# Layer 2 in token blocks of 1024 instead of 768

## The chip, the cores and the metric

One core of a Trainium2 chip. TensorE (PE) multiplies matrices and adds into the eight banks of PSUM, each 512 fp32 wide per partition; VectorE (DVE) and ScalarE (ACT) read PSUM and SBUF; GpSimd (POOL) works in SBUF; SyncE (SP) issues the DMAs. The metric is the device time of the whole program in microseconds, as the median of several runs.

## What is computed

A filter in the frequency domain, then two dense layers on the 6016 filtered tokens of 256 features. The change is in the second layer:

```python
y   = irfft(rfft(x, axis=1) * (filt_r + 1j * filt_i))     # (2, 3008, 256) -> 6016 tokens
h   = y @ w_in;   x2 = (h * sigmoid(h)) @ w_out           # layer 1: 256 -> 2048 -> 256
g   = x2 @ w_gate; v = x2 @ w_val                         # layer 2: 256 -> 1536, twice
out = (g * sigmoid(g) * v) @ w_out2                       # 1536 -> 256
```

Every fp32 operand is cut into a high and a low part (type fp32r), and a product is three matmuls: high·high, high·low, low·high.

## The kernel before

The program is written out instruction by instruction in Python; the engines keep that order, and semaphores and buffers follow from it. Layer 1 ends at about 640 us; the rest is layer 2.

Layer 2 walks over blocks of `STEP2` = 768 tokens (seven of them and one of 640), and in a block over six **units** (`Pair`, line 666), each with 256 hidden features of gate and value. In a unit, gate (`Gate` g) and value (v) are each computed by seven products instead of eight, on halves of the tokens and quarters of the weights: `p15` (products 1 and 5, into banks `a` and `b`), `p6` (into bank `y`), product 2 (onto `a`), `p3` (onto `b`), `p7` and `p4` (onto `y`). So a unit is 14 products, 42 matmuls (line 616) whose moving operand is half a block wide: 384 columns, or 320 in the last block. The order of a unit on PE is g1, g5, the p4 of the unit before's v, g6, g2, g3, g7, v1, v5, g4, v6, v2, v3, v7. Between them ACT copies `a` and `b` aside (lines 639, 641), takes Silu (690, 694, 699) and makes the high part of the hidden values `h` (711, 738); DVE adds and multiplies (647, 651, 656, 664, 686, 707, 709) and makes the low part of one half of them (714); POOL adds (660) and makes the low part of the other (739).

The hidden values go through `w_out2` in the **out products** (`m2_out`, line 744): one for each 128 tokens and part, 256 columns wide (line 756), added over the whole block in banks `acc`, two token tiles to a bank, so three banks for 768 tokens. They stand in a queue (`queue`), first in first out, and are dealt out evenly behind the matmuls of the products: `owed[1]` is the queue's length at the start of a unit over 42. The last unit of the program is dealt out at double rate in its second part, and `finish` (line 718) ends it in two halves.

All banks come from one pool of eight. With three for `acc`, five are left for `a`, `b` and `y` of the gates.

The operands of the products: `load_x2` reads a block, `prep_x2` makes four sums of its quarters on POOL (line 593), and `split_x2` makes high and low parts of seven operands on ACT and DVE (lines 606, 607), into ten buffers of the pool `late2`; the next block's are made while the last units of a block run. The general pool `mid` has 35 buffers of 4 KB per partition: weights, `h`, `s`, and so on.

```python
for k, (wpart, xpart) in enumerate(PARTS):
    nc.tensor.matmul(o, w_op(u, key, n, wpart), x[:, xpart, :size2(t) // 2], ...)
    owed[0] += owed[1]
    while owed[0] >= 1 and queue:
        owed[0] -= 1
        drain(len(queue) - 1)
```

Of the kernel before, what the change touches and what calls it, by code (L numbers as in the profile page):

```python
# [11 lines left out]
F32R = mybir.dt.float32r  # L12
# [16 lines left out]
P = 128  # L29
# [1 line left out]
NTOK = B * N  # L31
NBLK = -(-NTOK // 512)

STEP2 = 768
NBLK2 = -(-NTOK // STEP2)
CHUNK = 4 * N2

# [57 lines left out]
def fft_filter_mlp_kernel(  # L95
# [56 lines left out]
    def mid(shape, name, dtype=F32):  # L152
        return mp.tile(shape, dtype, tag="mid", name=name)
# [415 lines left out]
    xop, late2, x2_of = {}, {}, {}  # L569

    def size2(t):
        return min(STEP2, NTOK - STEP2 * t)

    def load_x2(t):

        r0, m = STEP2 * t, size2(t)
        xs = [mid([P, STEP2], "x2") for _ in range(2)]
        a = r0
# [10 lines left out]
    def prep_x2(t, part):  # L589

        x, n = x2_of[t], size2(t) // 2
        r = mid([P, 2, STEP2 // 2], "xr")
        sub = lambda o, a, b: nc.gpsimd.tensor_tensor(o, a, b, op=ALU.subtract)
# [8 lines left out]

    def split_x2(t, k):
        v, n = x2_of[t][k], size2(t) // 2
        x = late2["p"].tile([P, 2, STEP2 // 2], F32R, tag="x", name="xo", bufs=10)
        nc.scalar.copy(x[:, 0, :n], v)
        nc.vector.tensor_tensor(x[:, 1, :n], v, x[:, 0, :n], op=ALU.subtract)
        xop[t, k] = x
# [236 lines left out]
    for n, k in enumerate((1, 5, 6, 2, 3, 7, 4)):  # L845
        at(END1 - 8 + n, split_x2, 0, k)
# [11 lines left out]
    for t in range(1, NBLK2):  # L858
        u = 6 * t - 6
        later(u + 2, 0, load_x2, t)  # L860
        later(u + 3, 1, prep_x2, t, 0)
        later(u + 3, 3, prep_x2, t, 1)
        for k, n in ((0, 1), (1, 5), (3, 6)):
            later(u + 4, k, split_x2, t, n)

        for k, n in ((3, 2), (3, 3), (4, 7)):
            later(u + 5, k, split_x2, t, n)
        later(u + 6, 0, split_x2, t, 4)
# [241 lines left out]
```

## Time and profile before

| | us |
|---|---|
| median of 3 runs (1189.18 to 1190.61) | 1189.54 |
| span of the profiled execution | 1187.3 |
| PE busy in it | 1176.4 |
| DVE / ACT / POOL busy | 724.4 / 667.3 / 432.6 |

The profile page gives busy time by engine, the chain of work that ended last, and the costliest groups of instructions. The trace behind it is asked for stretches of time, for one engine's instructions in order, and for who waited for whom. PE's rows show a start that was measured and an end that is modelled, so that rows of matmuls overlap; from one start to the next is what a matmul costs.

### The profile page before, as it was taken

What the parts mean: (1) busy time and instruction counts of PE and PEld (TensorE: products, weight loads), DVE (VectorE), ACT (ScalarE), POOL (GpSimd) and SP (SyncE); (2) the same over time, 40 slices, a digit from 0 to 9 for tenths busy, and PEclk for the clock granted to TensorE, in tenths of its full rate; (3) what the DMA queues carried; (4) which work ended last, traced back from release to release, by engine and by line L of the source; (5) the groups of instructions that cost most, each with busy time, mean ns of one, the idle gap of its engine ahead of it and who ended that gap; (6) DMA issues with size and microseconds to landing.
All of it is one profiled execution on the core that took longest, in us unless ns stands there. A gap on an engine that the chain in (4) does not pass through costs nothing.

```text
span 1187.3 us, 17740 instructions
## 1 busy us (share of the span) xinstructions
PE 1176.4 (99%) x6646; PEld 1059.2 (89%) x6646; DVE 724.4 (61%) x1078; ACT 667.3 (56%) x1208; POOL 432.6 (36%) x341
## 2 busy tenths in 40 slices
PE   9999999999999999999999999999999999999998
PEld 7578788888888888888899999999999999999998
DVE  4778866763433433443345676767777676767766
ACT  3778766655565565656554554555545455454553
POOL 2556632420144134134211424334343343434332
PEclk9999999999999999999999999999999999999999
DMA  9883523313034232312563514242341434223230
GB/s 221 249 250 80 143 87 92 106 63 98 1 107 134 88 119 97 114 57 95 190 245 134 190 63 166 93 142 92 106 135 60 160 107 143 89 90 138 72 134 23
DMA packets 67574, 141.57 MB, mean 119 GB/s; under 512 B 5568, under 2 KB 32704, under 8 KB 67488
## 3 DMA queue, kind: packets, MB, share of 16 engines
q1 hardware_dynamic: 67488, 140.44, 36.8%
q8 instruction: 52, 0.85, 0.3%
q14 instruction: 34, 0.28, 0.1%
HBM read 104.50 MB, written 35.91 MB: 118 GB/s over the span
## 4 chain that ended last, share of the span: by engine, by line
PE 92%; DVE 2%; POOL 2%; ACT 2%; DMA 2%; issue 1%; SPq 0%; POOLq 0%; DVEq 0%; ACTq 0%
PE h L509 20%; PE acc L553 20%; PE acc L756 16%; PE y L616 13%; PE xa L616 8%; PE xb L616 8%; PE s L342 2%; PE s L175 2%; PE s L178 2%; DMA fr<-in_fr_dram 1%; DVE h L517 1%; DMA raw<-in_w_out_dram 1%; POOL fl L200 1%; POOL m L413 1%; PE s L229 1%
## 5 line engine op out<-in xcount | busy, mean ns | idle before, releaser
L756 PE MATMUL acc<-w,h 128*128 128x256 f32 x1692 | 465.5, 280 | 0.5 <-POOL h L714 0.2
L756 PEld LDWEIGHTS acc<-w,h 128*128 128x128 f32 x1692 | 316.0, 188 | 1.1 <-POOL h L714 0.4
L517 DVE TENSOR_TENSOR h<-u,h 128x512 fp32r<-128x512 f32 (+1 forms) x192 | 167.5, 876 | 244.7 <-ACT h L516 244.3
L553 PE MATMUL acc<-h,w 128*128 128x512 f32 (+1 forms) x1152 | 293.0, 387 | 1.8 <-ACT h L516 1.6
L509 PE MATMUL h<-xh,w 128*128 128x512 f32 (+1 forms) x768 | 269.5, 392 | 0.7 <-DVE xl L356 0.7
L553 PEld LDWEIGHTS acc<-h,w 128*128 128x128 f32 x1152 | 215.6, 188 | 45.9 <-ACT h L516 2.0
L536 ACT ACTIVATE u<-h 128x512 f32<-128x512 f32 (+1 forms) x192 | 112.8, 588 | 132.9 <-PE h L509 132.4
L616 PE MATMUL y<-xo,wst 128*128 128x384 f32 (+1 forms) x576 | 174.6, 336 | 0.0
L616 PE MATMUL xb<-xo,wst 128*128 128x384 f32 (+1 forms) x576 | 173.8, 335 | 0.0
L509 PEld LDWEIGHTS h<-xh,w 128*128 128x128 f32 x768 | 144.1, 188 | 30.5 <-DVE xl L356 1.2
L616 PE MATMUL xa<-xo,w 128*128 128x384 f32 (+1 forms) x576 | 164.1, 335 | 0.0
L660 POOL TENSOR_TENSOR c<-u,s 128x384 f32<-128x384 f32 (+1 forms) x95 | 97.5, 1026 | 173.5 <-DVE u L656 135.0
L739 POOL TENSOR_TENSOR h<-c,h 128x768 fp32r<-128x768 f32 (+1 forms) x47 | 85.8, 1826 | 176.2 <-ACT h L738 173.1
L509 PE MATMUL h<-xl,w 128*128 128x512 f32 (+1 forms) x384 | 149.2, 389 | 0.0
L516 ACT CAST h<-u 128x512 fp32r<-128x512 f32 (+1 forms) x192 | 117.5, 612 | 6.2
L616 PEld LDWEIGHTS y<-xo,wst 128*128 128x128 f32 x576 | 107.3, 188 | 0.8 <-DVE u L647 0.2
L616 PEld LDWEIGHTS xb<-xo,wst 128*128 128x128 f32 x576 | 107.4, 188 | 0.0
L616 PEld LDWEIGHTS xa<-xo,w 128*128 128x128 f32 x576 | 101.6, 188 | 0.0
L711 ACT CAST h<-ga 128x768 fp32r<-128x768 f32 (+1 forms) x48 | 39.5, 823 | 100.4 <-DVE ga L709 100.4
L664 DVE TENSOR_TENSOR c<-y,s 128x384 f32<-128x384 f32 (+1 forms) x96 | 52.1, 543 | 71.2 <-PE y L616 71.2
L509 PEld LDWEIGHTS h<-xl,w 128*128 128x128 f32 x384 | 72.1, 188 | 14.8
L714 DVE TENSOR_TENSOR h<-ga,h 128x768 fp32r<-128x768 f32 (+1 forms) x47 | 70.3, 1496 | 21.4 <-ACT h L711 21.4
(105 smaller groups left out, 1490.9 us busy)
## 6 DMA issues: line engine op xcount, KB each, us to landing
wst<-ds_g SPq DMA_DIRECT2D x48, 512.0 KB, 3.5
wst<-ds_v SPq DMA_DIRECT2D x48, 512.0 KB, 3.4
raw<-in_w_out_dram SPq DMA_DIRECT2D x14, 512.0 KB, 6.9
zt<-d SPq DMA_DIRECT2D x16, 384.0 KB, 5.2
x<-in_xp_dram SPq DMA_DIRECT2D x15, 384.0 KB, 8.8
d<-z SPq DMA_DIRECT2D x11, 512.0 KB, 3.9
d<-x SPq DMA_DIRECT2D x22, 256.0 KB, 2.2
out_dram<-ob SPq DMA_DIRECT2D x21, 256.0 KB, 2.2
```

The costliest lines, as they stand in the source:

```text
L509: nc.tensor.matmul(ps[:, :n], wt[key, f // 4, g][:, wpart, o:o + P], x[xpart][:, g, :n], start=(g == 0 and k == 0), stop=(g == 1 and k == 2),)
L516: nc.scalar.copy(h[:, 0, :n], u[:, :n])
L517: nc.vector.tensor_tensor(h[:, 1, :n], u[:, :n], h[:, 0, :n], op=ALU.subtract)
L536: nc.scalar.activation(u[:, :n], ps[:, :n], AF.Silu)
L553: nc.tensor.matmul(a[:, :n], w[:, wpart, o:o + 128], h[:, xpart, :n], start=(f == 0 and k == 0), stop=(f == 15 and k == 2),)
L616: nc.tensor.matmul(o, w_op(u, key, n, wpart), x[:, xpart, :size2(t) // 2], start=(first and k == 0), stop=(last and k == 2), skip_group_ch ...
L660: eng.tensor_tensor(self.c[:, self.n:], u3, self.s[:, 1], op=ALU.add)
L664: nc.vector.tensor_tensor(self.c[:, :self.n], self.y, self.s[:, 0], op=ALU.add)
L711: nc.scalar.copy(h[0], a[:, :m])
L714: eng.tensor_tensor(h[1], a[:, :m], h[0], op=ALU.subtract)
L739: nc.gpsimd.tensor_tensor(h[1], c, h[0], op=ALU.subtract)
L756: nc.tensor.matmul(a[:, D * (i % 2):D * (i % 2) + D], h[hpart][:, P * i:P * i + P], w[:, wpart, f % 2], start=(at_ == 0 and k == 0 and i % ...
```

## The change

`STEP2` becomes 1024, so layer 2 has five blocks of 1024 tokens and one of 896: 36 units instead of 48. Products become 512 columns wide (448 in the last block), and a block has four `acc` banks, so four banks are left for the gates. A buffer of `xo` grows from 3 KB to 4 KB; two of the seven operands (1 and 5) move to the pool `mid`, and `late2` keeps eight buffers. No other line changes; line numbers behind line 605 grow by three.

```diff
-STEP2 = 768
+STEP2 = 1024
...
     def split_x2(t, k):
         v, n = x2_of[t][k], size2(t) // 2
-        x = late2["p"].tile([P, 2, STEP2 // 2], F32R, tag="x", name="xo", bufs=10)
+        if k in (1, 5):
+            x = mid([P, 2, STEP2 // 2], "xo", F32R)
+        else:
+            x = late2["p"].tile([P, 2, STEP2 // 2], F32R, tag="x", name="xo", bufs=8)
```

**The first out products.** PE's order in the second unit of layer 2, before: `xa`, `xb` and `y` are the banks of the gates, `acc<-h` at line 553 is the end of layer 1, `acc<-w_5103,h` at line 756 the first out products, the second of which reads the low part of the first unit's `h`.

```order
L616 MATMUL xb<-xo,wst 128x384 x3
L616 MATMUL y<-xo,w_5080 128x384 x3
L553 MATMUL acc<-h,w 128x384
L616 MATMUL y<-xo,wst 128x384 x2
L553 MATMUL acc<-h,w 128x384
L616 MATMUL y<-xo,wst 128x384
L616 MATMUL xa<-xo,w_5039 128x384
L756 MATMUL acc_5569<-w_5103,h 128x256
L616 MATMUL xa<-xo,w_5039 128x384 x2
L756 MATMUL acc_5569<-w_5103,h 128x256
```

The same place now:

```order
L619 MATMUL xb<-xo,wst 128x512 x3
L619 MATMUL y<-xo,w_5080 128x512
L553 MATMUL acc<-h,w 128x384
L619 MATMUL y<-xo,w_5080 128x512 x2
L553 MATMUL acc<-h,w 128x384
L619 MATMUL y<-xo,wst 128x512
L759 MATMUL acc_5561<-w_5103,h 128x256
L619 MATMUL y<-xo,wst 128x512 x2
L759 MATMUL acc_5561<-w_5103,h 128x256
```

The second out product stands three products' matmuls earlier, behind 15 instead of 18 since the first unit's v3.

**The out products between the products.** PE in the middle of layer 2, before: one out product at most follows a product's matmul.

```order
L616 MATMUL xa<-xo,w_5686 128x384 x2
L756 MATMUL acc_7196<-w_5566,h 128x256
L616 MATMUL xa<-xo,w_5686 128x384
L756 MATMUL acc_7196<-w_5566,h 128x256
L616 MATMUL xb<-xo,wst 128x384
```

And now:

```order
L619 MATMUL y<-xo,w_5497 128x512
L759 MATMUL acc_7348<-w_5123,h 128x256 x2
L619 MATMUL y<-xo,w_5497 128x512
L759 MATMUL acc_7348<-w_5123,h 128x256
L619 MATMUL y<-xo,w_5497 128x512
```

A unit has 48 out products to 42 matmuls, where it had 36; six times a unit two out products follow each other.

**The end.** PE's last rows, before: `h` through `w_5762` is the last unit's first half, through `w_5827` from the fourth row on what `finish` makes.

```order
L756 MATMUL acc_11174<-w_5762,h 128x256 x6
L756 MATMUL acc_11175<-w_5762,h 128x256 x6
L756 MATMUL acc_11176<-w_5762,h 128x256 x3
L756 MATMUL acc_11175<-w_5827,h 128x256 x3
L756 MATMUL acc_11176<-w_5827,h 128x256 x3
L756 MATMUL acc_11174<-w_5827,h 128x256 x6
L756 MATMUL acc_11175<-w_5827,h 128x256 x3
```

And now, with seven token tiles instead of five:

```order
L759 MATMUL acc_9962<-w_5779,h 128x256 x6
L759 MATMUL acc_9963<-w_5779,h 128x256 x6
L759 MATMUL acc_9964<-w_5779,h 128x256 x6
L759 MATMUL acc_9965<-w_5779,h 128x256 x3
L759 MATMUL acc_9964<-w_5849,h 128x256 x6
L759 MATMUL acc_9965<-w_5849,h 128x256 x3
L759 MATMUL acc_9962<-w_5849,h 128x256 x6
L759 MATMUL acc_9963<-w_5849,h 128x256 x6
```

The last half of `h` is first read 30 out products behind the start of these rows, where it was 21.

## Rows read from the trace of the kernel before

**Rows 1.** Page: PE's busy time, and the chain that ended last, by engine.

```profile
PE 1176.4 (99%) x6646; PEld 1059.2 (89%) x6646; DVE 724.4 (61%) x1078; ACT 667.3 (56%) x1208; POOL 432.6 (36%) x341
...
PE 92%; DVE 2%; POOL 2%; ACT 2%; DMA 2%; issue 1%; SPq 0%; POOLq 0%; DVEq 0%; ACTq 0%
```

**Rows 2.** Waits of PE from 640 us: us in total, times, longest.

```profile
PE acc L756 <- POOL h L714: 0.2, 1, 0.2
```

**Rows 3.** Stretches of layer 1 and 2: length, busy (x instructions), granted clock, DMA.

```profile
300.00:590.00 290.00, 290.00 (x1333) 239.68 (x1332) 114.31 (x177) 175.07 (x312) 97.84 (x84) 1.00 0.30 98
...
700.00:1100.00 400.00, 400.00 (x2679) 398.69 (x2678) 286.80 (x451) 202.53 (x366) 157.38 (x128) 1.00 0.34 114
```

**Rows 4.** PE groups by shape, of 300 to 590 and 700 to 1100 us: busy, mean ns.

```profile
L342 PE MATMUL s<-cst,zt 96*128 96x94 f32 x136 | 17.5, 271 | 0.0
...
L756 PE MATMUL acc<-w,h 128*128 128x256 f32 x1236 | 345.3, 279 | 0.0
```

**Rows 5.** PE in order of time, layer 2: start us, modelled us.

```profile
799.88 0.28 PE L756 MATMUL acc<-w,h 128*128 128x256 f32 x1
800.00 0.34 PE L616 MATMUL y<-xo,wst 128*128 128x384 f32 x1
...
801.93 0.34 PE L616 MATMUL xb<-xo,wst 128*128 128x384 f32 x1
```

**Rows 6.** PE in order of time, layer 1: small matmuls, and 512 columns.

```profile
396.05 1.03 PE L342 MATMUL s<-cst,zt 96*128 96x94 f32 x8
396.87 0.48 PE L509 MATMUL h<-xh,w 128*128 128x512 f32 x1
...
500.08 0.40 PE L509 MATMUL h<-xh,w 128*128 128x512 f32 x1
500.31 1.53 PE L553 MATMUL acc<-h,w 128*128 128x512 f32 x6
```

**Rows 7.** PE in order of time, last block of layer 2, 320 columns.

```profile
1139.72 0.31 PE L616 MATMUL xb<-xo,wst 128*128 128x320 f32 x1
...
1141.20 0.31 PE L616 MATMUL xa<-xo,w 128*128 128x320 f32 x1
```

**Rows 8.** All engines in order of time, from unit 0's v3 to the second out product.

```profile
638.04 0.33 PE L616 MATMUL xb<-xo,wst 128*128 128x384 f32 x1
...
639.60 0.84 ACT L711 CAST h<-ga 128x768 fp32r<-128x768 f32 x1 [2.29 <-DVE ga L709]
...
640.47 1.54 DVE L714 TENSOR_TENSOR h<-ga,h 128x768 fp32r<-128x768 f32 x1 [0.44 <-ACT h L711]
...
642.25 0.28 PE L756 MATMUL acc<-w,h 128*128 128x256 f32 x1
```

**Rows 9.** Groups by shape from 860 us: busy us, mean ns of one.

```profile
L651 DVE TENSOR_TENSOR xb<-xb,u 128x384 f32<-128x384 f32 x44 | 24.8, 563 | 4.6 <-PE xb L616 2.9
...
L651 DVE TENSOR_TENSOR xb<-xb,u 128x320 f32<-128x320 f32 x12 | 6.0, 498 | 2.2 <-PE xb L616 2.2
```

**Rows 10.** All engines in order of time, the end.

```profile
1176.74 1.57 POOL L714 TENSOR_TENSOR h<-ga,h 128x640 fp32r<-128x640 f32 x1 [3.80 <-ACT h L711]
...
1177.00 1.66 DVE L727 TENSOR_TENSOR c<-c 128x320 f32<-128x320 f32 x1
1177.15 1.00 PE L756 MATMUL acc<-w,h 128*128 128x256 f32 x7
1178.37 4.54 PE L756 MATMUL acc<-w,h 128*128 128x256 f32 x29 [0.22 <-POOL h L714]
```

**Rows 11.** All engines in order of time, a unit from g3's last matmul on.

```profile
910.19 0.34 PE L616 MATMUL xb<-xo,wst 128*128 128x384 f32 x1
...
910.35 0.94 DVE L686 TENSOR_TENSOR c<-c 128x768 f32<-128x768 f32 x1
...
911.68 0.55 DVE L651 TENSOR_TENSOR xb<-xb,u 128x384 f32<-128x384 f32 x1
...
912.27 0.49 ACT L694 ACTIVATE ga<-xb 128x384 f32<-128x384 f32 x1
```

## The prediction

> **What bounds the kernel now.** I read the page first: PE is busy for 99% of the span, and the chain that ended last is 92% PE [rows 1]. Busy PE alone proves little, because the ends of matmuls are modelled; so next the waits: from 640 us to the end PE waited once, for 0.2 us [rows 2]. Then the stretches: between 700 and 1100 us PE is never idle, at the full granted clock of 1.00, while DVE, ACT and POOL are busy for 287, 203 and 157 of 400 us [rows 3]. Layer 2 is bound by the rate at which PE starts matmuls. A change gains there only what it takes off PE, and loses whatever makes PE wait.
>
> **Part 1: fewer, wider product matmuls.** The number of columns stays; the number of matmuls falls. Before: 42 units of 42 matmuls at 384 columns (1764) and 6 units at 320 (252). After: 30 units at 512 (1260) and 6 at 448 (252). That is 504 fewer, so all hangs on what a matmul costs beyond its columns.
>
> An out product first: between 799.88 and 801.93 seven of them stand, and their starts and the starts behind them are 0.82 us apart in sum, 0.117 us each [rows 5]. Then a 384: 700 to 1100 us holds 2679 matmuls [rows 3], of which 1236 are out products [rows 4]; (400 - 1236 x 0.117) / 1443 = 0.177 us. A 320: from 1139.72 to 1141.20 there are six of them and five out products [rows 7]: (1.48 - 0.585) / 6 = 0.149 us. Is there a fixed part? A product matmul with one out product takes 2.05 / 7 = 0.293 us at 384 columns, since seven of each lie between 799.88 and 801.93 [rows 5], and (1.48 + 0.117) / 6 = 0.266 at 320 [rows 7]: 0.027 us for 64 columns, 0.42 ns a column. By that slope the 640 columns of a pair account for 0.267 of its 0.293 us, and 0.013 us of each matmul are fixed. A pair with 512 columns would take 0.293 + 128 x 0.00042 = 0.346, the 512 of it 0.229.
>
> Layer 1 has matmuls of 512 columns: 300 to 590 us holds 1333 matmuls [rows 3], 136 of them small ones [rows 4]; eight of these take from 396.05 to 396.87, 0.10 us each [rows 6]. (290 - 13.9) / 1197 = 0.231 us. Four thirds of 0.177 would be 0.236. The two groups of layer 1 differ: the six of line 553 have (1.53 - 0.39) / 5 = 0.228 between starts, the step of line 509 is 0.23 [rows 6]. I take the mean, 0.231 and not 0.229, since it holds the small waits that 0.177, a mean too, also holds, and keep 0.228 and, just short of four thirds, 0.235 as ends. A 448 is put half way between 384 and 512: 0.204 (ends 0.202 and 0.206).
>
> Before: 1764 x 0.177 + 252 x 0.149 = 312.2 + 37.5 = 349.7 us. After: 1260 x 0.231 + 252 x 0.204 = 291.1 + 51.4 = 342.5 us. **-7.2 us**; with the ends -11.5 and -1.7.
>
> A page of notes speaks against the change. The Trainium skill ("TensorE: Matmul & The Clock Gate", section "Back-to-back issue gap") gives N / 2.4 + 2.5 ns for the step of a warm matmul; by that rule 504 matmuls fewer are an estimated 1.3 us instead of 7.2. The rows here disagree: their fixed part is 13 ns.
>
> **Part 2: out products behind each other.** Their number stays at 1692, but six times a unit two now stand in a row, in all some 200 pairs more. In the end of the program they do so already: seven take 1.00 us, the last with a modelled 0.28 [rows 10], so 0.72 / 6 = 0.120 instead of 0.117. 200 x 0.003 = **+0.6 us** (0 to +0.6: the products' mean takes in rows that are cheaper next to them).
>
> **Part 3: the second unit.** The second out product needs the low part of the first unit's `h`. Before, the last matmul of v3 ends at 638.04 + 0.17 = 638.21; DVE and ACT make `ga` and its high part, and DVE ends the low part at 640.47 + 1.54 = 642.01 (3.80 us behind v3), and PE needs it at 642.25 [rows 8]: 0.24 to spare, hidden by 18 product matmuls. Now PE comes there after 15 product matmuls, four of layer 1 and one out product: 15 x 0.231 + 4 x 0.175 + 0.12 = 4.3 us. The chain grows. Line 651 and its like take 0.50 us at 320 columns and 0.56 at 384 [rows 9], so 0.69 at 512, twice 0.13 more; line 714's 1.54 and the cast's 0.84 [rows 8] grow by at most a third, 0.51 and 0.28, and I take 0.42 and 0.22, since they too have a fixed part. 3.80 + 0.26 + 0.42 + 0.22 = 4.7 us. PE waits **+0.4 us**, once (0 to +0.7). What stands behind it on PE is the whole program.
>
> **Part 4: inside a unit, and between blocks.** A product with its out products took 3 x 0.177 + 36/14 x 0.117 = 0.83 us and takes 3 x 0.231 + 48/14 x 0.117 = 1.09 us, 1.31 times as much. The work between products grows by at most 4/3, and DVE's by 0.69 / 0.56 = 1.23, because each instruction has a fixed part too. So every wait whose place did not move has the same room or more. What moved are the banks: a new `a`, `b` or `y` takes the bank of the fourth before it, not the fifth. I went through the six tiles of a unit in the order; the one with the least room is v6, which takes the bank of g's `b`. That bank is free when the Silu of line 694 has read it: 910.19 + 0.17 to 912.27 + 0.49, 2.4 us behind g3 [rows 11], at most 2.4 x 4/3 = 3.2 now. Between g3 and v6 lie g7, v1, v5 and g4: 4 x 1.09 = 4.4 us. **0**, with 1.2 us to spare. At the change of a block four new `acc` banks are wanted, and three come from gates that were read long before, the fourth is an old `acc` bank, first written 18 out products behind the last write of the old ones; copying it is one instruction on ACT. 0. Two operands in `mid`: their buffers were given back a unit and more earlier in the order, and a block's loads are four DMAs as before. 0; if the cover were gone, each operand that comes late costs what is missing of it, once a block. The weights are loaded 36 times instead of 48.
>
> **Part 5: the end.** Before, PE loses time there: 29 out products take 4.54 us where 28 x 0.12 + 0.28 = 3.64 would do, and the seven ahead of them end 0.38 us before the 29 start [rows 10]. The reason is a row: DVE's line 727 takes 1.66 us beside POOL's 1.57 us [rows 10], where DVE's 320 columns take about 0.5 [rows 9]; behind it the last `h` is late. Now POOL's line 714 is 896 wide, at 1.57 x 7/5 = 2.2 us at most, and the four DVE steps behind it take 0.12 longer each, some 1.3 us later in all; but PE has 30 instead of 21 out products ahead of that `h`, 9 x 0.12 = 1.1 us, and more ahead of the POOL step. **0**, between -0.5 and +0.8: two more DMAs are issued at the end.
>
> **Sum:** -7.2 + 0.6 + 0.4 + 0 + 0 = -6.2 us. On the profiled 1187.3 that is 1181.1; the median of the runs lies 2.2 above the span, so 1183.3. With the ends of part 1 and the other bounds together -12.0 to +0.4: 1177.5 to 1189.9.
>
> **Rivals.**
>
> *The fixed part is gone at 512 columns.* If a 512 costs four thirds of a 384, 0.236, with a 448 at 0.2065, the products take 297.4 + 52.0 = 349.4 and gain 0.3; with the small losses 1189.54 - 0.3 + 1.0 = 1190.2, no change. For it: 0.231 is nearer to 0.236 than to 0.213, which 512 columns would take at 0.42 ns with no fixed part. Against: the mean over 1197 matmuls, and the slope between 320 and 384 columns. Chance 0.13. The rule of the Trainium skill named above comes out beside it, at an estimated 1189.2.
>
> *Four banks are too few.* If the Silu that frees g's `b` is not done within 4.4 us behind g3, PE stops at v6 in every unit. The point is 1.2 us of delay above my 3.2. A row shows what could do it: an instruction of DVE held up beside POOL, 1.66 for 0.5 us [rows 10], 1.2 us more, and 1024 wide POOL's step would take 1.57 x 8/5 = 2.5 us. A hold of 2 us would bring the chain to 5.2, 0.8 us a unit, 35 x 0.8 = 28 us: 1211. Against: in the order POOL's long step waits for the cast behind line 686 and so does not start ahead of it, and at 910.35 line 686 ran in 0.94 [rows 11]. Chance 0.09.
>
> **How the numbers follow.** Forecast 0.78. About 0.2% (2.4 us) is what a measurement of this kernel tells from no change: faster means below 1187.2, slower above 1191.9. The upper end of the forecast's own range reaches into no change for a few parts in a hundred. Faster 0.76, same 0.14, slower 0.10. The range 1178.5 to 1189.3 takes in nearly all of the forecast and half of the first rival.
>
> **What would show it.** In the profile after: line 619 in steps of about 0.231 us at 512 columns; in a stretch of the middle of layer 2 PE busy all the time and a unit of 42 x 0.231 + 48 x 0.118 = 15.4 us; one wait of PE for DVE's line 717 at about 0.4 us near 641 us; waits near the end of about 1 us in all. I would be wrong if PE shows waits for line 697, 710 or 712 (banks) or for 609 or 610 (operands) that come back with every unit or block, or if the steps at 512 columns are 0.236.

## The result, and the profile after

| | before | after |
|---|---|---|
| median, us | 1189.36 (4 runs, 1189.12 to 1190.61) | 1180.45 (4 runs, 1180.12 to 1181.34) |
| ratio, 95% interval | | 0.9919 [0.9893, 0.9946] |
| span of the profiled execution, us | 1187.3 | 1178.9 |

The change is faster by 8.9 us, 0.8%; 1183.3 with a range of 1178.5 to 1189.3 was forecast. The page of the changed kernel (span; busy time; chain that ended last), which answers to [rows 1]:

```profile
span 1178.9 us, 16278 instructions
...
PE 1167.9 (99%) x6142; PEld 994.7 (84%) x6142; DVE 708.1 (60%) x921; ACT 652.1 (55%) x1086; POOL 425.5 (36%) x297
...
PE 90%; DVE 3%; DMA 2%; ACT 2%; POOL 2%; issue 1%; SPq 0%; POOLq 0%; DVEq 0%; ACTq 0%
```

PE has 504 matmuls fewer, its busy time is 8.5 us shorter, and it is still 99% of the span. The same two stretches as in [rows 3], and all waits of PE behind 630 us (total, times, longest), which answer to [rows 2]:

```profile
300.00:590.00 290.00, 290.00 (x1333) 239.61 (x1332) 114.40 (x177) 174.72 (x312) 97.83 (x84) 1.00 0.30 98
700.00:1100.00 400.00, 400.00 (x2365) 354.51 (x2364) 280.42 (x349) 194.88 (x286) 151.35 (x95) 1.00 0.27 90
```

```profile
PE acc L759 <- DVE h L717: 0.3, 1, 0.3
PE acc L759 <- DVE h L732: 0.3, 1, 0.3
PE y L619 <- DVE u L659: 0.2, 1, 0.2
```

Layer 1 is what it was. In layer 2 PE is busy throughout at the full granted clock, and the weight loads (PEld), 399 of 400 us before, now leave gaps. No wait comes back with a unit or a block: L717 is the second unit's, the other two stand at the end. PE in order of time in the middle of layer 2 (start, modelled us), which answers to [rows 5]:

```profile
906.00 0.27 PE L759 MATMUL acc<-w,h 128*128 128x256 f32 x1
906.11 0.40 PE L619 MATMUL y<-xo,wst 128*128 128x512 f32 x1
906.34 0.28 PE L759 MATMUL acc<-w,h 128*128 128x256 f32 x1
906.46 0.39 PE L619 MATMUL y<-xo,wst 128*128 128x512 f32 x1
906.69 0.27 PE L759 MATMUL acc<-w,h 128*128 128x256 f32 x1
```

From one out product to the one two rows on it is 0.34 and 0.35 us: the pair that the prediction put at 0.346. Nothing but starts is read here; the modelled 0.40 us of a 512 overlap the next row.

**Where the 8.5 us went.** I summed the steps between PE's starts from the first product of layer 2 to PE's last matmul: 554.1 us before, 545.6 after, and what lies around that stretch differs by 0.2. A step that is over 25 ns longer than the median of its kind is counted as a wait, also where the view of waits shows none.

| us | predicted | measured | how |
|---|---|---|---|
| product steps | -7.2 | -5.5 | medians: 1764 x 0.175 + 252 x 0.149 = 346.2; 1260 x 0.230 + 252 x 0.202 = 340.7 |
| waits at block starts | not priced | -2.0 | 23 long steps before: 21 at the seven later blocks' starts (1.8 us), 2 in the second unit; none of these after |
| out products' own steps | +0.6 | -1.2 | below |
| second unit | +0.4 | +0.6 | wait for line 717 |
| end | 0 | -0.1 | 1.58 us of long steps before, 1.44 after |
| sum (with rest) | -6.2 | -8.5 | -8.2, and -0.3 between medians and means of the product steps |

Without the steps counted as waits, and by means, the product steps are 5.8 us shorter in sum and the out products' 1.3 us: 7.0 us together, 14 ns for each of the 504 matmuls left out.

The waits at block starts are hidden in the rows of before. One of them, PE and DVE in order of time:

```profile
906.50 0.55 DVE L656 TENSOR_TENSOR u<-y,s 128x384 f32<-128x384 f32 x1
906.64 0.28 PE L756 MATMUL acc<-w,h 128*128 128x256 f32 x1
...
906.94 0.28 PE L756 MATMUL acc<-w,h 128*128 128x256 f32 x1
907.10 0.44 PE L616 MATMUL y<-xo,w 128*128 128x384 f32 x1
...
907.38 0.28 PE L756 MATMUL acc<-w,h 128*128 128x256 f32 x1
```

The step at 906.94 is 0.16 instead of 0.117 and the next 0.28 instead of 0.175: the first matmul of p4 adds onto the bank `y` that DVE's line 656 reads until 907.05. Three and a half us later g7 loses 0.11 in the same way behind line 647. The view of waits is silent, since the modelled end of one matmul covers the gap to the next. In the blocks of 768 tokens the first unit of a block took 11.86 us and every other 11.62, from the fourth unit on; after, 26 units from the fourth of layer 2 on take 15.28 each, first of a block or not.

### The profile page after: what moved, and what is told of

It is laid out like the page before. It is cut to its first block, busy times and chain, and to the rows that moved or that the text cites. A ratio compares the mean times of both kernels' runs of the same rounds, so it can differ in the third digit from the quotient of the medians.

```text
span 1178.9 us, 16278 instructions
## 1 busy us (share of the span) xinstructions
PE 1167.9 (99%) x6142; PEld 994.7 (84%) x6142; DVE 708.1 (60%) x921; ACT 652.1 (55%) x1086; POOL 425.5 (36%) x297
## 4 chain that ended last, share of the span: by engine, by line
PE 90%; DVE 3%; DMA 2%; ACT 2%; POOL 2%; issue 1%; SPq 0%; POOLq 0%; DVEq 0%; ACTq 0%
PE h L509 20%; PE acc L553 20%; PE acc L759 16%; PE y L619 12%; PE xa L619 8%; PE xb L619 8%; PE s L342 2%; PE s L178 2%; PE s L175 1%; DMA x<-in_xp_dram 1%; DMA fr<-in_fr_dram 1%; DVE h L517 1%; POOL fl L200 1%; POOL m L413 1%; PE s L229 1%
## 5 line engine op out<-in xcount | busy, mean ns | idle before, releaser
L759 PE MATMUL acc<-w,h 128*128 128x256 f32 x1692 | 434.2, 280 | 0.7 <-DVE h L717 0.3
L619 PE MATMUL xa<-xo,w 128*128 128x512 f32 (+1 forms) x432 | 156.2, 388 | 0.0
L663 POOL TENSOR_TENSOR c<-u,s 128x512 f32<-128x512 f32 (+1 forms) x71 | 92.7, 1305 | 173.7 <-DVE u L659 94.9
L619 PE MATMUL xb<-xo,wst 128*128 128x512 f32 (+1 forms) x432 | 154.1, 388 | 0.0
L619 PE MATMUL y<-xo,wst 128*128 128x512 f32 (+1 forms) x432 | 153.9, 388 | 0.0
L742 POOL TENSOR_TENSOR h<-c,h 128x1024 fp32r<-128x1024 f32 (+1 forms) x35 | 83.0, 2370 | 172.0 <-ACT h L741 172.0
L667 DVE TENSOR_TENSOR c<-y,s 128x512 f32<-128x512 f32 (+1 forms) x72 | 48.5, 674 | 78.2 <-PE y L619 78.2
L619 PEld LDWEIGHTS y<-xo,wst 128*128 128x128 f32 x432 | 80.6, 187 | 15.7
L714 ACT CAST h<-ga 128x1024 fp32r<-128x1024 f32 (+1 forms) x36 | 37.2, 1033 | 96.7 <-DVE ga L712 96.7
L619 PE MATMUL y<-xo,w 128*128 128x512 f32 (+1 forms) x216 | 79.8, 388 | 0.2 <-DVE u L659 0.2
```

The costliest lines, as they stand in the source:

```text
L663: eng.tensor_tensor(self.c[:, self.n:], u3, self.s[:, 1], op=ALU.add)
L667: nc.vector.tensor_tensor(self.c[:, :self.n], self.y, self.s[:, 0], op=ALU.add)
L714: nc.scalar.copy(h[0], a[:, :m])
L742: nc.gpsimd.tensor_tensor(h[1], c, h[0], op=ALU.subtract)
L759: nc.tensor.matmul(a[:, D * (i % 2):D * (i % 2) + D], h[hpart][:, P * i:P * i + P], w[:, wpart, f % 2], start=(at_ == 0 and k == 0 and i % ...
```

## The experiments

Ten kernels, each against the kernel before on the same chip.

**Does a price of each matmul explain the gain?** Of the changed kernel, the third matmul of each product is cut into halves: 512 columns and four banks stay, the number of matmuls goes back to 2016.

```diff
-nc.tensor.matmul(o, ..., x[:, xpart, :size2(t) // 2], ...)
+m = size2(t) // 2
+for a, b in ((0, m // 2), (m // 2, m)) if k == 2 else ((0, m),):
+    nc.tensor.matmul(o[:, a:b], ..., x[:, xpart, a:b], ...)
```

> The changed kernel, but the third matmul of every product (low weights by high operand) is issued as two matmuls of half the columns: 504 matmuls more, the number before the change, with the blocks of 1024, four banks and all else kept. Theory (the gain is the fixed part of a matmul, 11 to 13 ns): 504 x 0.011 to 0.013 = 5.5 to 6.6 us slower than the changed kernel's 1180.4, so 1186 to 1187, with a pair of 256 columns in 0.235 to 0.24 us where 512 take 0.231. Rival 1 (the gain came from waits that went, at the starts of blocks and at the end, and the number of matmuls costs next to nothing): within 1.5 us of 1180.4. Rival 2 (proportional to columns, 0.236 for four thirds of 0.177): no difference either.

Measured: 1192.7, ratio to before 1.0023 [1.0006, 1.0040]. The whole gain goes, and 3 us more: 24 ns a matmul, twice what was expected. By steps: the halves take 0.120 us each, +4.9 us, near what was expected, but the uncut matmuls beside them cost 4.6 us and the out products 2.8 us more. PE there, a product with its last matmul cut:

```profile
911.68 0.39 PE L621 MATMUL y<-xo,wst 128*128 128x512 f32 x1
911.91 0.28 PE L761 MATMUL acc<-w,h 128*128 128x256 f32 x1
912.02 0.40 PE L621 MATMUL y<-xo,wst 128*128 128x512 f32 x1
912.27 0.28 PE L761 MATMUL acc<-w,h 128*128 128x256 f32 x1
912.39 0.40 PE L621 MATMUL y<-xo,wst 128*128 128x256 f32 x2
912.63 0.40 PE L761 MATMUL acc<-w,h 128*128 128x256 f32 x2
```

The two halves together take 0.24 us, from 912.39 to 912.63. Of the two uncut 512s the first takes 0.23 and the second, after which the halves come, 0.25; in the mean of 352 between 700 and 1100 us the second takes 0.239, the first 0.233. The view of waits shows none that was not in the changed kernel.

**All of them cut**, the same edit for every k:

> The changed kernel with every product matmul cut in two: 1512 matmuls more. Theory (fixed part): three times the first run's loss, 1512 x 0.011 to 0.013 = 16.6 to 19.7 us slower, 1197 to 1200. Rivals (waits, or proportional to columns): 1180 to 1184.

Measured: 1201.7, ratio 1.0094 [1.0063, 1.0126]: 14 ns for each of 1512 more. All matmuls of layer 2's full blocks now take 0.120 us, products and out products alike. That is just above the range expected (1197 to 1200). Of the 14 ns, 9 stand in the cut matmuls' own steps and 5 in the out products, which go from 0.116 to 0.120 us in the mean. So each matmul more costs here what each matmul less gave back in the change, 14 ns; the first run's 24 ns are not that price.

**Does the place matter?** The first matmul of each product cut instead of the third (`k == 0`):

> The changed kernel with the first matmul of each product cut in halves instead of the third: 504 matmuls more, as many narrow ones, in another place. Cut in the third, the run took 1192.7, 24 ns a matmul, and the 512 ahead of the halves had taken 0.241 us in 250 cases instead of 0.23. Theory (a price of each matmul, wherever it stands): 1192.7 again. Rival (the price beyond 13 ns comes from the row of narrow matmuls that halves and the out product behind them make, and goes when the halves stand elsewhere): 1187.

Measured: 1194.0, ratio 1.0040 [1.0025, 1.0054], 27 ns each. This doesn't decide between theory and rival, since the edit hardly moves the halves. With the third matmul cut, PE's row is 512, out product, 512, out product, half, half, out product, and then the same again; with the first cut it is half, half, out product, 512, out product, 512, out product: the same ring, entered at another place. In both, the halves stand between two out products, and in both the 512 ahead of that row takes 0.239 us. In the run with all cut, nothing but narrow matmuls carries no surcharge (0.120 each), but whether a row of them between 512s does is untested.

**Is there a smallest step?** The third matmul cut unevenly, first with 128 columns at the end, then 64 (`(0, m - 128), (m - 128, m)`):

> The changed kernel with the third matmul of each product cut unevenly, into all columns but the last 128 and these 128: again 504 matmuls more, as in the run with halves, which took 1192.7 where a fixed part of 11 to 13 ns allowed 1186 to 1187. Theory 1 (a matmul costs 13 ns and 0.42 ns a column at every width): the 128 take 0.067 us, the run is between 1186 and 1193. Theory 2 (a matmul has a smallest step, near the 0.117 to 0.120 us that all matmuls of 256 columns show, set by the weight load that goes with each): the 128 take about 0.11 to 0.12, the pair 384 + 128 takes 0.29 instead of 0.23, 504 x 0.05 to 0.06 = 25 to 32 us: 1206 to 1213.

> As the run with the cut into all but 128 columns and 128, but with the last 64 cut off. That run took 1214.6: the 128 took 0.060 us, but the out product behind them 0.171 instead of 0.117, so that both together took 0.231, twice 0.115; rows of weight loads stood 0.10 apart there at the closest, and the next matmul started 0.12 behind its load. Theory (a weight load of about 0.115 us goes with each matmul, and a matmul narrower than that leaves the rest to the one behind it): 64 columns and the out product again take 0.231, the 448 take 0.202, so the third matmul costs 0.202 + 0.114 = 0.316 instead of 0.231, 504 x 0.085 = 43 us and the 4 that went elsewhere in the run with 128: 1227. Rival (what was lost belongs to the 128 columns themselves and shrinks with them, or each cut has one price): 1214 or less.

Measured: 1214.6 (ratio 1.0214 [1.0201, 1.0227]) and 1225.3 (1.0305 [1.0288, 1.0322]). The smaller the piece, the dearer: 68 and 89 ns for each of the same 504 more. One price for each cut is out, and so is theory 1. PE with 128 columns, in order of time:

```profile
909.20 0.40 PE L621 MATMUL xa<-xo,w 128*128 128x384 f32 x2
909.43 0.33 PE L761 MATMUL acc<-w,h 128*128 128x256 f32 x1
909.60 0.40 PE L621 MATMUL xb<-xo,wst 128*128 128x512 f32 x1
```

and with 64:

```profile
908.83 0.41 PE L621 MATMUL y<-xo,w 128*128 128x448 f32 x2
909.08 0.36 PE L761 MATMUL acc<-w,h 128*128 128x256 f32 x1
909.27 0.39 PE L621 MATMUL y<-xo,wst 128*128 128x512 f32 x1
```

The piece itself starts its successor after 0.060 or 0.030 us, not 0.11 to 0.12 as theory 2 had it, but the out product behind it then takes 0.171 or 0.198 (means) instead of 0.117: both together 0.231 and 0.228, about as much as two of 256. The weight loads of the first stretch, one for each matmul:

```profile
909.08 0.31 PEld L621 LDWEIGHTS xa<-xo,w 128*128 128x128 f32 x2
909.38 0.19 PEld L761 LDWEIGHTS acc<-w,h 128*128 128x128 f32 x1
909.48 0.19 PEld L621 LDWEIGHTS xb<-xo,wst 128*128 128x128 f32 x1
```

The load for the out product starts at 909.38, and the out product 0.06 behind it. The load for the 512 starts 0.11 behind the load ahead of it (0.108 to 0.110 in all 345 such places from 700 to 1100 us; the rows are rounded), and its matmul 0.12 behind that, at 909.60. In layer 2 of no run do two loads start closer than 0.107 us. This load starts 0.05 behind the out product; in the changed kernel a load starts 0.003 behind the matmul ahead of its own (mean). A narrow matmul and the one behind it thus take two such steps, some 0.115 us each, and what the narrow one is short of that stands in its neighbour's step. The Trainium skill ("TensorE: Matmul & The Clock Gate", section "LDWEIGHTS (loading the stationary operand)") gives columns / 1.2 ns for a load, an estimated 107 ns for these 128 columns. The 0.108 us between loads agree. No kernel here has a matmul without its load, so that the load sets the step, and not something else that goes with each matmul, is inferred and not shown.

**A size between.** `STEP2 = 896`, all else as changed (36 units of 448 columns, 6 of 320):

```diff
-STEP2 = 1024
+STEP2 = 896
```

> The changed kernel with blocks of 896 tokens: 36 units of 448 columns and 6 of 320, 1764 product matmuls; before had 2016, after has 1512; banks and operand tiles as after. Theory (each product matmul left out gives back the same, some 8.9 us for 504 together with the small waits at block starts): half of the way, 1184.5 to 1185.5. Worked from the steps of the two traces: 1512 x 0.202 + 252 x 0.149 = 343.0 us of products, 2.3 more than after's 340.7 at the same kind of step; six block starts instead of five at no wait: 1182.8 to 1184.5. Rival (the banks and the place of the operands, not the size, gave the gain): 1180.5, as after. Rival (the waits at block starts come back with seven blocks): 1186 or more, and PE waits for lines 647 to 662 in the waits.

Measured: 1184.1, ratio 0.9957 [0.9942, 0.9972], inside the figures worked from the steps (1182.8 to 1184.5), a little over half of the way. The interval, some 1.8 us to either side, doesn't tell these from the half-way figure, but rules out 1180.5, the rival by which banks and placement gave the gain. Without the long steps, products and out products are 3.6 us shorter here than before for 252 matmuls fewer: 14 ns each again. The waits at block starts have shrunk, not gone: the first unit of a block takes 13.52 us, every other 13.44. So they fall with the width, from 0.24 us a block to 0.08 to none. The rows fit a race: from 384 to 512 columns a unit grows 1.31 times (11.62 to 15.28 us), the DVE steps that the waiting matmuls need 1.25 times (lines 647 and 656 before, 0.55 us; lines 650 and 659 after, 0.69 us).

**Is it the placement of the operands?** The kernel before, with only the pool change:

```diff
-x = late2["p"].tile([P, 2, STEP2 // 2], F32R, tag="x", name="xo", bufs=10)
+if k in (1, 5):
+    x = mid([P, 2, STEP2 // 2], "xo", F32R)
+else:
+    x = late2["p"].tile([P, 2, STEP2 // 2], F32R, tag="x", name="xo", bufs=8)
```

> The kernel before, with only the second part of the change: operands 1 and 5 in the general pool and eight buffers for the others, blocks of 768 kept. Theory: no difference, within 0.5 us of 1189.4, PE without new waits; each buffer was given back a unit or more ahead. Rival (operands in the general pool come late or hold up the loads): waits of PE for lines 609 or 610 at each of seven block changes, 1 to 5 us slower.

Measured: 1188.8, ratio 1.0002 [0.9982, 1.0021], and the same long steps at the block starts (first unit of each). This part gives and costs nothing that the interval, 2 us to either side, or the steps would show.

**Can the waits at block starts be had apart?** The kernel before, with two of the splits for the next block one place earlier:

```diff
-for k, n in ((3, 2), (3, 3), (4, 7)):
+for k, n in ((2, 2), (2, 3), (4, 7)):
     later(u + 5, k, split_x2, t, n)
```

> The kernel before, with the splits of operands 2 and 3 of the next block moved from behind v6 to ahead of v6 in a block's last unit. In the kernel before PE loses about 0.25 us at the start of each of seven blocks: the u of the old v (line 656) and of the new g (line 647) are late on DVE, since these two splits stand on it ahead of line 707. Theory (that is part of the gain: in the changed kernel those waits are gone, because DVE's steps grew 1.23 times and PE's 1.31): without the splits in that place the waits go in the kernel before too, 1.7 us faster, 1187.7. Rival (the waits come from elsewhere, or move to line 647 of v): within 0.5 us of 1189.4.

Measured: 1195.5, ratio 1.0052 [1.0040, 1.0063], slower by 6 to 7 us. All waits of PE from 640 us, and one of them on PE, with the next block's p4 (`y<-xo,w`) behind it:

```profile
PE y L616 <- DVE u L647: 6.2, 7, 1.2
PE acc L756 <- POOL h L714: 0.2, 1, 0.2
```

```profile
906.83 0.28 PE L756 MATMUL acc<-w,h 128*128 128x256 f32 x1
908.00 0.44 PE L616 MATMUL y<-xo,wst 128*128 128x384 f32 x1 [0.88 <-DVE u L647]
...
910.50 0.28 PE L756 MATMUL acc<-w,h 128*128 128x256 f32 x1
910.62 0.34 PE L616 MATMUL y<-xo,w 128*128 128x384 f32 x1
910.79 0.28 PE L756 MATMUL acc<-w,h 128*128 128x256 f32 x1
```

The step is 1.17 instead of 0.117 us: the two splits now stand ahead of v's line 647, and the product behind it waits a full microsecond once a block. The rival's place was right and its price too low. But the old waits are gone. The steps at 910.50 and 910.62 are 0.12 and 0.17, where before the same two were 0.16 and 0.28; the first unit of each block now takes 11.62 us like every other, and the last unit of a block 12.75 instead of 11.62. That fits the theory, but doesn't prove it: PE now comes to the block's start 1.1 us later, and that alone gives DVE the time that it lacked. So the waits are DVE's lateness at that place; that these two splits make it late is not shown, and no kernel removed the waits at 768 tokens without a larger one elsewhere. Their 1.8 us are read from the trace.

**How far are four banks from too few?** The changed kernel with one bank held through layer 2 by one small matmul whose result is read at the end, so three are left for the gates:

```diff
+hold = psum("hold")
+nc.tensor.matmul(hold[:, :256], idle[:, :P], idle, start=True, stop=True)
...
+nc.vector.tensor_copy(z[:, :256], hold[:, :256])
```

> The changed kernel with one bank of PSUM held through all of layer 2 by a tile that is written once and read at the end, so that three banks are left for a, b and y. Theory (four banks are enough, with room; the release of a bank sets when the next tile starts): g6 then follows the read of the old y directly and v6 that of g's y, each read some 0.25 + 0.69 us behind its product, so two waits of about 1 us a unit: 36 x 2 = 70 us slower, 1240 to 1260, with PE waiting for line 667. Rival (banks already are what paces layer 2, hidden in the steps): a loss that is spread over all matmuls, without single waits of 1 us.

Measured: 1243.1 (one run), inside the theory's 1240 to 1260. PE's largest wait, and one stop in order of time:

```profile
PE y L619 <- DVE c L667: 43.6, 58, 1.8
```

```profile
906.11 0.28 PE L759 MATMUL acc<-w,h 128*128 128x256 f32 x1
907.05 0.50 PE L619 MATMUL y<-xo,wst 128*128 128x512 f32 x1 [0.67 <-DVE c L667]
```

Most units take 17.36 us instead of 15.28. With five banks (before) and four (after) no such wait is there; the next bank less costs 63 us. That is what the rival of the prediction would have looked like.

**The second unit's wait.** The changed kernel, with the dealing in that unit held back a little longer:

```diff
-owed[0], owed[1] = 0.0 if self.u != 1 else -3.0, (len(queue) + 1e-6) / 42
+owed[0], owed[1] = 0.0 if self.u != 1 else -5.0, (len(queue) + 1e-6) / 42
```

> The changed kernel, with the first out products of the second unit dealt out later (the dealing starts at -5 instead of -3, so the second out product stands behind 13 product matmuls of its unit instead of 9). Theory (PE waits there once, 0.5 us and 0.1 us for the matmul behind it, for the low part of h): the wait for line 717 near 645 us is gone and the span is 0.6 us shorter, 1179.8 by the median. Rival (the out products put off come back as a wait at the end or in the next unit): no difference.

Measured: 1179.8, ratio to before 0.9912 [0.9882, 0.9943], 0.64 below the changed kernel. PE's waits behind 630 us are now the two at the end:

```profile
PE acc L759 <- DVE h L732: 0.3, 1, 0.3
PE y L619 <- DVE u L659: 0.2, 1, 0.2
```

It is the fastest of all, though 0.6 us against the changed kernel is less than the intervals tell apart; that the wait has gone is what the trace shows.

## Why the prediction came out right, step by step

**The bound** was right: PE's starts set the time, and fewer products shortened it.

**Part 1** reads best and is half right. 342.5 us of products were forecast and 342.6 measured; 349.7 was taken for before and 349.4 measured. But 0.177 was a mean over a stretch in which PE never showed idle, and it was taken for the price of a matmul. The prediction said that its means hold small waits, and set the 0.231 of layer 1 beside the 0.177 as if both held alike; they didn't. Of the 0.177, 0.175 is the step, and 1.6 of the 2.0 us of long steps at block starts and in the second unit lie in products (0.4 in out products). Part 4 gave waits the same room or more at a price of 0, and no term priced waits that go: that part of the -7.2 is luck. With median steps the term is -5.5, or 11 ns for each of 504 matmuls, near the 13 of the fixed part. The rest of the 14 ns stands in the out products, which part 2 took the other way. The choice of 0.231 over 0.235 was borne out: median 0.230, mean 0.231. By the rule that the prediction weighed, N / 2.4 + 2.5 ns (the Trainium skill, "TensorE: Matmul & The Clock Gate", section "Back-to-back issue gap", which gives it for an isolated matmul), a 512 would be an estimated 0.216. The measured step disagrees, and so do the 14 ns for each matmul.

**Part 2** had the sign wrong. Where two out products stand in a row they do cost more, 0.117 and 0.119 us; but alone behind a 512 an out product takes 0.1160 (mean of 1028), where behind a 384 it took 0.1176 with 0.0002 of waits in it. Together -1.2 instead of +0.6. The term's bounds, 0 to +0.6, left no room for a gain, though no row excluded one.

**Part 3** held in its mechanism and nearly in its size. DVE's low part and the product that waits, all engines in order of time, which answers to [rows 8]:

```profile
642.21 1.05 ACT L714 CAST h<-ga 128x1024 fp32r<-128x1024 f32 x1 [2.77 <-DVE ga L712]
...
643.29 2.00 DVE L717 TENSOR_TENSOR h<-ga,h 128x1024 fp32r<-128x1024 f32 x1 [0.52 <-ACT h L714]
...
645.34 0.39 PE L759 MATMUL acc<-w,h 128*128 128x256 f32 x1 [0.34 <-DVE h L717]
```

The cast took 1.05 (forecast 1.06) and line 717 2.00 (1.96); v3's last product starts at 640.31, so the chain from its end to 645.29 is 4.75 us (4.7). PE lost 0.50 at the step ahead of it and 0.11 at this one (0.4), at 644.6 to 645.6 and not near 641 as forecast. The run with the dealing held back gives the 0.6 back.

**Part 4**, no waits for banks or operands: right, by PE's waits above, by the units' even 15.28 us (15.4 forecast), and by the run with the pool change alone. The run with three banks shows what the rival's wait costs.

**Part 5**, the end: right within 0.1 us, by a balance that was only roughly right. All engines, the end, which answers to [rows 10]:

```profile
1166.50 2.19 POOL L717 TENSOR_TENSOR h<-ga,h 128x896 fp32r<-128x896 f32 x1 [5.24 <-ACT h L714]
...
1166.82 2.36 DVE L730 TENSOR_TENSOR c<-c 128x448 f32<-128x448 f32 x1
...
1167.11 5.56 PE L759 MATMUL acc<-w,h 128*128 128x256 f32 x42
...
1172.94 1.58 PE L759 MATMUL acc<-w,h 128*128 128x256 f32 x11 [0.28 <-DVE h L732]
```

POOL's step took the 2.2 us forecast, and DVE's line 730 beside it 2.36 instead of 1.66; it ends at 1169.18, with POOL's at 1168.69. Three waits of 0.5, 0.3 and 0.6 us are left where there were four, 1.4 us in all where about 1 was forecast, and the longer row of out products (42 in a row against 29) covers what DVE's step takes more. The prediction's 0.38 us at the old kernel's end is what the step before the 29 takes over 0.12; by the modelled end in [rows 10] the seven end 0.22 us ahead.

**The rivals.** A 512 at four thirds of a 384 is out: 0.230 against 0.236, or 0.233 from the 0.175 of a step without waits; the product steps would then hardly be shorter in sum, and they are, by 5.5 to 5.8 us. Too few banks is out at four, and real at three.

**What stays open:** why a layer 2 in which a third of the wide matmuls is halved costs 24 to 27 ns for each cut, some 15 more than the halves' own steps, with some uncut 512s at 0.239, when halving all of them costs 14. The smallest step of some 0.115 us does not explain it, since no matmul in the full blocks is narrower than 256 columns there. Open too is why out products are cheaper beside wider matmuls.

## What to carry to other kernels

Where PE starts a matmul as soon as the one before lets it, price an edit by the steps between starts, kind by kind, and compare their median with their mean: a mean over a stretch without idle time can hold waits that no view lists, and they go or stay for reasons of their own. Every matmul left out of this stream gave back some 14 ns, part of it in its neighbours' steps, and a piece of 128 or 64 columns saved nothing against one of 256. Before calling one experiment a check of another, write out the order on the engine that both give: two edits can make the same one. Before taking a bank or buffer away, find the tile with the least room; one bank was free here, and the next cost 63 us.

## What the runs showed of the hardware

- Steps of fp32r matmuls with a weight load each, at a granted clock of 1.00: 0.230 us at 512 columns, 0.202 at 448, 0.175 at 384, 0.149 at 320, 0.117 to 0.120 at 256. From 320 to 512 that is 0.42 ns a column and some 14 ns fixed. In layer 2 of all runs, weight loads start 0.107 us apart at the closest.
- At 128 and 64 columns the step itself is 0.060 and 0.030 us, but the next matmul pays: it and the narrow one together take 0.231 and 0.228 us. The cost of a narrow matmul stands in its neighbour's row.
- DVE's 448 columns took 2.36 us (line 730) beside POOL's line 717, and 0.62 us when the same line ran again at 1171.00 without it.
